# Loading the main part of wq in eight transfers of sixteen partitions instead of one of 128

## The chip, the cores and the metric

The kernel runs on one core of a Trainium2 chip. The metric is the device time of one execution in microseconds (us); for the kernel before it is 1275.67 us (median of 3 runs, 1275.54 to 1275.78). A change of 0.2% of that is 2.55 us.

## The reference

One token is decoded. It goes through a grouped-query attention over a long cache and, beside it, through a gated feed-forward block; a scalar gate mixes the two.

```python
x = A_x                                              # 1 x 1 x 448, bf16
g = _sigmoid((x * gate_w).sum(-1, keepdims=True))
a = _A_ref(x, k_cache, v_cache, wq, wo)              # 16 query heads of 256, 8 KV heads, 65536 positions
b = _B_ref(x, W_gate, W_up, W_down)                  # (relu(x W_gate) * (x W_up)) W_down, F = 1792
return g * a + (1 - g) * b
```

In `_A_ref` the queries are `q = x @ wq` (448 x 4096), then follow the scores against the K cache, a softmax over 65536 positions, the sum over the V cache and the product with `wo`. K and V are 8 x 65536 x 256 in bf16 each, 268 MB apiece. All weights together are some 12 MB.

## The kernel before, in words

All work is listed as operations with a key, an engine and the operations that they depend on (`_Plan`, the functions `op` and `dma`). Each engine runs its own operations in the order of their keys; `finish` turns the dependencies into waits on semaphores. Every engine has one counting semaphore; every DMA names one, which each transfer raises by 16, so an operation that depends on a transfer waits for the number that the semaphore has after that transfer.

The keys of the loads come from the list `order`, written out by hand, with a planned duration for each entry: wq, then the feed-forward weights, then the first K tile, then W_down, then K tiles and, from the fourth on, V tiles in turn; near the end the last V tiles in halves and pieces between the parts of wo. A K or V tile is 128 partitions x 64 KB, 8 MB, and there are 32 of each. They go through three buffers, `ring[0]` to `ring[2]`. A load is issued by SP (its DMA queue is q1 in the profile) and waits there until what its buffer held before has been used (`free`).

The weights of the start lie in the same buffers. `ring[2]` holds, per partition, three rows of wq (`wq3`, 24 KB), three rows of W_gate and three of W_up (10.5 KB each) and halves of the last rows of both; `ring[1]` holds the last 64 rows of wq as half rows (`wqa`, 4 KB per partition). With R3 = 3 and NR3 = 384, partition p of `wq3` holds the rows 3p, 3p+1 and 3p+2 of wq, which are contiguous in HBM.

The loads of the start are issued by two engines. SP issues, in this order: wq's main part (line 614), wq's rest (615), the rest of W_up (line 275), the first K tile into `ring[0]` (673). Behind these stands W_down (662), which waits for the queries, because it goes into the part of `ring[2]` that holds wq; the second K tile (`ring[1]`) waits for the queries too, the third (`ring[2]`) for the feed-forward block. ACT issues W_gate's main part (271), x (273), gate_w (274), the rest of W_gate (275) and W_up's main part (277) into its own queue, q10.

The queries are computed on TensorE. `f_q` (16 passes over three rows per partition, 48 matmuls) depends on the wq transfer (`l_["wq"]`), on x in its transposed form and, since operations that share a PSUM bank are kept in the order of their keys (`serialize`), on the scalar gate before it. The gate is a chain of small operations over POOL, DVE, ACT and PE that begins when x has landed. `f_q2` then adds the part of `wqa`. ACT copies the result, DVE transposes it and ACT builds `xm`, the stationary operand of all score matmuls.

In the main part DVE transposes each K tile in place (line 454), PE multiplies it with the queries (line 373, tile ST), DVE takes the maximum, ACT the exponentials, and after four tiles of a head the probabilities are rescaled and transposed and multiply the V tiles (line 373, tile O).

Of the kernel before, what the change touches and what calls it, by code (L numbers as in the profile page):

```python
# [25 lines left out]
class _Plan:  # L26
# [13 lines left out]
    def dma(self, eng, key, sem, fn, deps=()):  # L40
        if sem not in self.dsem:
            self.dsem[sem] = self.es.enter_context(self.nc.semaphore("d_" + sem))
        o = _Op(eng, key, fn, deps, dma=sem)
        self.ops.append(o)
        return o
# [66 lines left out]
def bass_gated_mix__gqa_block_cached__glu_gated_reglu__decode_kernel(  # L112
# [24 lines left out]
    R3 = D // 128  # L137
    NR3 = R3 * 128
# [13 lines left out]
    with es:  # L152
# [43 lines left out]
        wq3 = ring[2][:, 0:R3 * NQ]  # L196
# [21 lines left out]
        op, dma = pl.op, pl.dma  # L218
# [26 lines left out]
        t = 3.0  # L245
# [238 lines left out]
        l_, qk, smax, aexp, pv, last = {}, {}, {}, {}, {}, {}  # L484
# [126 lines left out]

        for kind, i, t in issue:
            if kind == "wq":
                l_["wq"] = dma("sp", t, "wq", lambda e: e.dma_start(wq3, A_wq[0:NR3, :].rearrange("(p k) n -> p (k n)", k=R3)))
                l_["wqh"] = dma("sp", t + 0.01, "wqh", lambda e: e.dma_start(
                    wqa, A_wq[NR3:D, :].rearrange("r (c n) -> (r c) n", c=2)))
                d_wh1 = dma("sp", t + 0.02, "wfh1", half(1, B_W_up))
# [8 lines left out]
            elif kind == "gu":  # L626
                t = tL["gu", 0]
# [41 lines left out]
            elif kind == "k":  # L669
                n = i  # L670
# [44 lines left out]
            elif kind in ("v", "vh", "vp"):  # L715
                if kind == "v":
                    n, lo, hi = i, 0, U
# [107 lines left out]
```

## Time and profile before

| | before |
|---|---|
| median of the runs | 1275.67 us |
| the profiled execution: its time | 1275.64 us |
| the profiled execution: its span | 1274.2 us |
| busy PE / DVE / ACT / POOL, share of the span | 29% / 51% / 5% / 3% |
| moved by DMA | 549.20 MB, mean 431 GB/s over the span |
| time of the packets of q1 / q10, share of 16 DMA engines' span | 99.2% / 0.6% |
| wq's main part, 3072 KB: issue to landing | 13.2 us |
| first K tile's issue by SP | at 2.11 us |
| first query matmuls on PE | at 18.20 us |

The span is the time from the first to the last instruction of the profiled execution on the core, and positions in it are given in us from its start. A row of the view of windows shows, for one stretch of the span, the busy time of each engine, the clock granted to PE, the share of the time that the core's 16 DMA engines were busy, and the rate at which they moved bytes. A packet is counted with its whole duration in the stretch in which it starts, so a stretch shorter than a few packets can show a share above 1. In the timeline, SPq and ACTq are the engines that issue transfers, with the duration of issuing one.

### The profile page before, as it was taken

To read this page: it belongs to the slowest core of one execution; us is meant where nothing else is said; L and a number is where in the kernel's file an instruction comes from. 1 tells how busy PE (TensorE), PEld (TensorE's weight loads), DVE (VectorE), ACT (ScalarE), POOL (GpSimd) and SP (SyncE) were. 2 spreads that over 40 slices of the span, in tenths; PEclk is the share of its full clock that TensorE was granted. 3 is DMA by queue.
4 is the path that set the end of the run, shared out by engine and by line. 5 is a ranking of instruction groups with operands and counts; after the bars stand their busy time and mean duration, and the time that the engine had idled before them with its cause. 6 is when DMAs were issued, how large, how long until landed. Compare 5 with 4: busy or idle time off the path is not lost.

```text
span 1274.2 us, 9555 instructions
## 1 busy us (share of the span) xinstructions
PE 371.4 (29%) x4483; PEld 105.0 (8%) x2909; DVE 648.7 (51%) x171; ACT 58.2 (5%) x112; POOL 37.2 (3%) x94
## 2 busy tenths in 40 slices
PE   4413222323133331224220342311332203223154
PEld 2101000101000000001000010000100000000010
DVE  1797633566534655445555454556535565336511
ACT  0000000000000000000000000000000000000000
POOL 2000000000000100001000010000100001000010
PEclk9566666656666665665656676556766556666577
DMA  9999999999999999999999999999999999999998
GB/s 414 429 444 428 426 428 430 447 438 428 428 432 428 442 435 434 428 434 428 441 434 434 428 434 430 439 434 434 428 438 428 436 434 434 430 438 428 436 421 378
DMA packets 11522, 549.20 MB, mean 431 GB/s; under 512 B 1267, under 2 KB 1654, under 8 KB 2422
## 3 DMA queue, kind: packets, MB, share of 16 engines
q1 hardware_dynamic: 11072, 546.05, 99.2%
q10 hardware_dynamic: 438, 2.98, 0.6%
q8 instruction: 8, 0.13, 0.0%
q14 instruction: 4, 0.03, 0.0%
HBM read 549.03 MB, written 0.00 MB: 431 GB/s over the span
## 4 chain that ended last, share of the span: by engine, by line
DMA 42%; DVE 32%; PE 16%; another core or an unknown queue 7%; issue 1%; POOL 0%; ACT 0%; SPq 0%; ACTq 0%
DMA ring<-in_A_k_cache_dram 34%; DVE ring L454 27%; PE ST L373 9%; PE O L373 5%; DMA ring<-in_A_v_cache_dram 4%; DMA ring<-in_A_wo_dram 3%; DVE P L701 1%; DVE P L699 1%; PE M_ps L373 1%; DVE o_sb L497 1%; DMA P<-in_A_x_dram 1%; DVE nmb L680 1%; PE ST L403 0%; PE M_ps L694 0%
## 5 line engine op out<-in xcount | busy, mean ns | idle before, releaser
L454 DVE STREAM_TRANSPOSE ring<-ring 128x16384 uint32<-128x16384 uint32 (+1 forms) x36 | 552.3, 15345 | 318.9 <-DMA ring<-in_A_k_cache_dram 318.9
L403 PE MATMUL ST<-nil_t,identb 1*128 1x1 bf16 x32 | 5.1, 158 | 767.6 <-DVE ring L454 767.6
L373 PE MATMUL ST<-ring,xm 128*16 x2048 | 185.2, 537 | 4.6 <-issue 0.7
L373 PE MATMUL O<-ring,P 128*32 x2016 | 133.9, 425 | 20.8 <-DMA ring<-in_A_v_cache_dram 18.3
L680 DVE TENSOR_REDUCE nmb<-ST 128x1 f32<-128x512 f32 x32 | 22.0, 688 | 185.0 <-PE ST L373 185.0
L682 ACT ACTIVATE P<-ST,nmb 128x512 bf16<-128x512 f32 x32 | 45.2, 1413 | 1082.8 <-DVE nmb L680 1082.8
L373 PEld LDWEIGHTS ST<-ring,xm 128*16 x2048 | 61.5, 112 | 115.2 <-issue 101.5
L403 PEld LDWEIGHTS ST<-nil_t,identb 1*128 1x128 bf16 x32 | 3.2, 100 | 792.6 <-issue 792.6
L497 DVE CAST_PREDICATED o_sb<-bm,O 128x512 bf16<-128x512 uint16 (+1 forms) x33 | 22.3, 679 | 69.2 <-PE O L356 46.9
L690 POOL TENSOR_TENSOR hs<-selc,hs 128x2 f32<-128x2 f32 x8 | 1.6, 196 | 1143.7 <-DVE hs L688 1143.7
L373 PEld LDWEIGHTS O<-ring,P 128*32 x504 | 15.7, 113 | 112.9 <-issue 110.4
L699 DVE TENSOR_TENSOR P<-P,hs 128x2048 bf16<-128x2048 bf16 x8 | 18.3, 2292 | 8.1 <-ACT hs L696 8.1
L702 POOL TENSOR_TENSOR hs<-hs,rs 128x4 f32<-128x4 f32 x8 | 18.4, 2305 | 13.6 <-ACT hs L696 13.6
L701 DVE STREAM_TRANSPOSE P<-P 128x2048 bf16<-128x2048 bf16 x8 | 18.5, 2311 | 0.3
L707 PE MATMUL M_ps<-hs,ones_f 128*128 128x2 f32 x16 | 4.7, 364 | 30.3 <-POOL hs L706 30.3
L373 PE MATMUL M_ps<-ring,P 128*128 x64 | 13.0, 341 | 1.5 <-PE M_ps L373 0.3
L525 PE MATMUL M_ps<-emat,o_sb 128*64 128x2 bf16 x48 | 3.0, 185 | 22.0 <-ACT o_sb L507 22.0
L682 ACT ACTIVATION_READ_ACCUMULATOR P<-ST,nmb 128x1 f32 x32 | 8.4, 263 | 0.0
L373 PEld LDWEIGHTS M_ps<-ring,P 128*128 x64 | 7.5, 119 | 6.9 <-issue 5.3
L336 DVE CAST xT<-M_ps 128x5 bf16<-128x5 f32 x1 | 0.2, 167 | 14.7 <-PE M_ps L324 14.7
L622 DVE STREAM_TRANSPOSE P<-P 128x128 uint32<-128x128 uint32 x1 | 0.3, 311 | 12.7 <-ACT P L621 12.7
L707 PEld LDWEIGHTS M_ps<-hs,ones_f 128*128 128x128 f32 x16 | 4.0, 312 | 30.9 <-POOL hs L706 30.9
(103 smaller groups left out, 94.0 us busy)
## 6 DMA issues: line engine op xcount, KB each, us to landing
ring<-in_A_v_cache_dram SPq DMA_DIRECT2D x3, 4096.0 KB, 28.9
ring<-in_A_v_cache_dram SPq DMA_DIRECT2D x2, 2048.0 KB, 36.3
ring<-in_A_wq_dram SPq DMA_DIRECT2D x1, 3072.0 KB, 13.2
ring<-in_A_wo_dram SPq DMA_DIRECT2D x1, 1792.0 KB, 19.6
ring<-in_B_W_down_dram SPq DMA_DIRECT2D x1, 1568.0 KB, 10.1
ring<-in_B_W_gate_dram ACTq DMA_DIRECT2D x1, 1344.0 KB, 13.4
ring<-in_B_W_up_dram ACTq DMA_DIRECT2D x1, 1344.0 KB, 26.5
ring<-in_A_wo_dram SPq DMA_DIRECT2D x1, 896.0 KB, 40.3
```

The costliest lines, as they stand in the source:

```text
L373: return e.add_instruction(mybir.InstMatmult(name=nc.get_next_instruction_name(), engine=e.engine, ins=[v, w], outs=[e.lower_ap(o)], start ...
L403: e.matmul(o, identb[0:1, :], nil_t[0:1, 0:1], start=True, stop=False, skip_group_check=True)
L454: return lambda e: e.transpose(v, v)
L497: return e.copy_predicated(dst, m.to_broadcast(list(src.shape)), src)
L525: ins = e.matmul(T_ps[p0:p0 + 64, s:c1 + 1:c1 - s], t[:, c:c + 64], emat2[:], start=(s == 0), stop=False, skip_group_check=True, tile_posi ...
L680: smax[n] = op("dv", tk + 26, lambda e, n=n, NM=NM, t_=t_: e.tensor_reduce(NM[:, t_:t_ + 1], ST[n % 2][:], AX.X, ALU.max, negate=True), [q ...
L682: aexp[n] = op("ac", tk + 27, lambda e, n=n, t_=t_, NM=NM, RS=RS, Ph=Ph: e.activation(Ph[:, t_:2048:4], ST[n % 2][:], ACTF.Exp, bias=NM[:, ...
L690: h2 = op("gp", T + 13.55, lambda e, X=X: e.tensor_tensor(X[:, 2:4], selc[:, 2:4], X[:, 0:1].to_broadcast([128, 2]), ALU.mult), [h1, g_sel])
L699: rsc = op("dv", T + 16, lambda e, X=X, pb=pb: e.tensor_tensor(pb, pb, X[:, 12:16].unsqueeze(1).to_broadcast([128, 512, 4]), ALU.mult), [h ...
L701: last["ev", h] = [op("dv", T + 17, lambda e, Ph=Ph: e.transpose(Ph[:], Ph[:]), [rsc])]
L702: l0 = op("gp", T + 18, lambda e, X=X, RS=RS: e.tensor_tensor(X[:, 16:20], X[:, 12:16], RS[:], ALU.mult), [h7])
L707: l3 = mop("pe", T + 19, lambda e, X=X: e.matmul(LS_ps, ones_f[:, :], X[:, 6:8], start=True, stop=True), [l2, c_one])
```

## The change

The transfer of wq's main part is replaced by eight. Transfer b (0 to 7) fills the sixteen partitions b, b+8, ..., b+120 of `wq3`, each with its same 24 KB from HBM. Their keys are 0.001 apart and lie ahead of the key of the next transfer, so SP issues all eight, one behind the other, before wq's rest. All eight raise the semaphore `wq`; `l_["wq"]` is the last of them, so the query matmuls wait until the semaphore has reached 128 instead of 16. Places, bytes and all other operations stay as they are.

```diff
             if kind == "wq":
-                l_["wq"] = dma("sp", t, "wq", lambda e: e.dma_start(wq3, A_wq[0:NR3, :].rearrange("(p k) n -> p (k n)", k=R3)))
+                wqs = A_wq[0:NR3, :].rearrange("(a b k) n -> a b (k n)", b=8, k=R3)
+                for b in range(8):
+                    l_["wq"] = dma("sp", t + 0.001 * b, "wq", lambda e, b=b: e.dma_start(wq3[b:128:8, :], wqs[:, b, :]))
                 l_["wqh"] = dma("sp", t + 0.01, "wqh", lambda e: e.dma_start(
                     wqa, A_wq[NR3:D, :].rearrange("r (c n) -> (r c) n", c=2)))
                 d_wh1 = dma("sp", t + 0.02, "wfh1", half(1, B_W_up))
```

## The prediction

> **What bounds the kernel now.** I began with the page's parts 2 and 3, to see whether anything but the transfers can set the end.
>
> ```profile
> DMA  9999999999999999999999999999999999999998
> GB/s 414 429 444 428 426 428 430 447 438 428 428 432 428 442 435 434 428 434 428 441 434 434 428 434 430 439 434 434 428 438 428 436 434 434 430 438 428 436 421 378
> ...
> q1 hardware_dynamic: 11072, 546.05, 99.2%
> q10 hardware_dynamic: 438, 2.98, 0.6%
> ```
>
> The 16 DMA engines are busy in every slice, and the packets of SP's queue (q1) and ACT's queue (q10) fill 99.8% of their time. The view of windows then shows where the remainder lies: the columns end with the DMA share and the GB/s.
>
> ```profile
> 0.00:1.70 1.70, 0.00 (x0) 0.00 (x0) 0.00 (x0) 0.00 (x0) 1.17 (x8) 1.00 0.00 0
> 1.70:3.60 1.90, 0.00 (x0) 0.00 (x0) 0.00 (x0) 0.63 (x1) 1.59 (x8) 1.00 0.89 252
> 3.60:12.80 9.20, 0.00 (x0) 0.00 (x0) 0.00 (x0) 0.66 (x1) 4.81 (x19) 1.00 1.00 431
> ...
> 100.00:1200.00 1100.00, 297.44 (x3795) 82.23 (x2422) 574.78 (x129) 49.21 (x92) 24.35 (x49) 0.62 1.00 433
> 1.70:1271.50 1269.80, 370.57 (x4473) 104.72 (x2901) 648.30 (x170) 57.85 (x111) 36.02 (x87) 0.63 1.00 432
> ```
>
> Nothing moves before 1.70 us, and from there to 1271.50 the share is 1.00. So the kernel is one unbroken stream of bytes with 1.7 us ahead of it and about 2.7 us behind it (1274.2 - 1271.5). A microsecond that the stream gains or loses anywhere, the start included, is a microsecond of the kernel, as long as the queues never run empty. The rate is also the same for very different rows: 431 GB/s where the rows of wq (24 KB) and W_gate (10.5 KB) run side by side, 433 where all are K and V rows of 64 KB. That is 26.9 GB/s for each engine (431 / 16), whatever the length: some fixed path is full, and row count or row length does not matter.
>
> SP's waits show what keeps the stream fed, and the timeline shows the issues at the start.
>
> ```profile
> SPq L719 <- PE ST L373: 912.1, 29, 36.0
> SPq L673 <- PE O L373: 156.7, 27, 13.9
> ...
> SPq L662 <- PE M_ps L373: 29.9, 1, 29.9
> ```
>
> ```profile
> 0.73 0.41 ACTq L271 DMA_DIRECT2D ring<-in_B_W_gate_dram  x1
> 0.74 0.38 SPq L614 DMA_DIRECT2D ring<-in_A_wq_dram  x1
> 1.18 0.42 SPq L615 DMA_DIRECT2D ring<-in_A_wq_dram  x1
> 1.64 0.42 SPq L275 DMA_DIRECT2D ring<-in_B_W_up_dram  x1
> 2.11 0.58 SPq L673 DMA_DIRECT2D ring<-in_A_k_cache_dram  x1
> ...
> 13.88 0.42 POOL L330 COPY P<-P 1x64 bf16<-1x64 bf16 x2 [4.28 <-DMA P<-in_A_x_dram]
> 18.20 7.94 PE L373 MATMUL M_ps<-ring,P 128*128 x48 [0.15 <-issue]
> 32.65 0.33 SPq L662 DMA_DIRECT2D ring<-in_B_W_down_dram  x1
> ```
>
> SP waits 29.9 us for the queries before it can issue W_down. That is the one place near the change where the stream could run dry. The next rows give the bytes ahead of it.
>
> ```profile
> ring<-in_A_wq_dram SPq DMA_DIRECT2D x1, 3072.0 KB, 13.2
> ring<-in_B_W_gate_dram ACTq DMA_DIRECT2D x1, 1344.0 KB, 13.4
> ring<-in_B_W_up_dram ACTq DMA_DIRECT2D x1, 1344.0 KB, 26.5
> ring<-in_A_wq_dram SPq DMA_DIRECT2D x1, 512.0 KB, 14.6
> ring<-in_B_W_up_dram SPq DMA_DIRECT2D x1, 224.0 KB, 18.0
> ring<-in_B_W_gate_dram ACTq DMA_DIRECT2D x1, 224.0 KB, 14.0
> ring<-in_B_W_down_dram SPq DMA_DIRECT2D x1, 1568.0 KB, 10.1
> ```
>
> The six loads ahead of W_down and the first K tile (8192 KB) are 14912 KB, 15.27 MB, or 35.4 us at 431 GB/s. The start lost 1.70 us and then 0.79 us (1.90 x (1 - 252/431)), so this stock lasts to 37.9 us. W_down is issued at 32.65, and by the first row of wq (issued 0.74, bytes at 1.7) its bytes can begin about 1.0 us later, at 33.7. The slack is 4.2 us.
>
> **The change part by part.**
>
> Issues. Seven more transfers on SP. One costs 0.44 to 0.47 us from start to start (0.74, 1.18, 1.64, 2.11), so wq's rest, W_up's rest and the first K tile are issued 3.1 to 3.3 us later, the K tile at about 5.4. What hides it: the stock of wq and W_gate rows, 4416 KB or 10.5 us of stream, ends near 13 us, well behind 5.4. The transfers of wq come fast enough too: an engine works through one of its wq rows and one W_gate row in 1.31 us (35328 B at 26.9 GB/s), SP brings the next in 0.47. Nothing else stands in SP's queue before 32.65. Cost 0; without that cover it would be 3.3 us. ACT's queue is untouched.
>
> Completion. Seven more completions per engine. The page has no row for one; from below it is 0, from above I take the whole gap between the stream's 432 GB/s and the slices' best 447, 3.4%, over wq's 7.3 us, which is 0.25 us. Most of that gap will have other reasons; I take 0.05.
>
> First rows. Each engine's first row ran at a reduced rate: share 0.89, but 252 GB/s. A transfer of 16 rows may be handed out to the engines sooner than one of 128. From below 0 (ACT's 128 rows are handed out at the same moment and the first row comes as late); from above all 0.79 us are won back. I take 0.2.
>
> The rows' own rate. This is the term that decides. [...] Every large transfer of the trace fills 128 partitions, so no row shows a store to a selection. The bounds are: no change, 0; and half rate, where the selection reaches only half of the paths and two rows share one, with wq's 3072 KB (3.146 MB) taking 14.6 us instead of 7.3, so +7.3. I take +7.3, nearer to what the rows tell of busy engines: in 1.70:3.60 they are 89% busy and yet move 252 of 431 GB/s, so an engine can be held up by something outside itself, and the same full-path rate for all row lengths is what a fixed store side would give. A gain by the selection has no row that speaks for it, since the rate is already the full one.
>
> [...]
>
> What is late next, if wq's rows take twice as long: an engine alternates between its two queues, so W_gate, and x behind it, are late as well. x lands 7.3 later at most, the gate chain that follows it (13.88 to 18.20) moves along, and the queries and W_down's issue with them, to 40.0. But the stock of bytes is late by the same 7.3, to 45.2, so the slack of 4.2 stays and adds nothing. If x were not late, wq's landing at about 21.2 would start the queries, 3.0 us later than now, with more slack still. The later loads have far more: the second K tile is issued right behind W_down, with 3.7 us of W_down ahead of it.
>
> Sum, against the profiled execution's 1275.64: +7.3 +0.05 -0.2 = 1282.8 us. The median of 1275.67 is 0.03 off that execution, which does not matter.
>
> **The rivals.**
>
> A, the selection costs nothing, because the engines alone are the full path. For it: 431 GB/s is 26.9 per engine in every stretch. Against: an engine can be busy and slow (252). Time 1275.64 + 0.05 - 0.2 = 1275.5, with bounds 1274.9 (all of 0.79 won back) and 1275.9. This is the side on which the kernel is not slower.
>
> [...]
>
> C, sharing leaves the engines uneven. Each landing counts when its last engine is through, and equal work afterwards does not even the lag out. If the last engine lags the mean by one doubled row (24576 B at half of 26.9 GB/s, 1.8 us), 1284.6.
>
> D, a transfer of sixteen rows does not run on sixteen engines. On eight, each would carry twice its rows of wq, so the time is +7.3 as well, but the DMA share would drop towards 0.5 in the stretch of wq. Nothing speaks for it: x's single small row tells nothing of its engines.
>
> **How the numbers follow.** About 0.2% (2.55 us) is what a measurement of this kernel can tell from no change. Half rate: 0.58, own range 1281.5 to 1284. A: 0.22. B: 0.08. C: 0.08. D: 0.02. The rest, 0.02, is left for a start that gains over 2.55 us in some way that I do not see. So faster 0.02, same 0.22 (A), slower 0.76. The range reaches from 1275.0, close to A's lower bound, to 1285.0, just beyond C; one sign holds most of the chance, but A is too likely to be left out.
>
> **What would show it.** In the stretch 3.60:12.80 the share stays 1.00 and the rate falls to about 254 GB/s (35328 B x 16 in 1.31 + 0.91 us); wq's landing moves from 13.9 to about 21, the queries from 18.2 to 21 to 25.5, W_down's issue to 36 to 40, and from 100 on everything runs at the old rate, shifted by 7. The rate back at 431 in that stretch shows A, a share well below 1 shows D or a hole from SP's issues, and zero windows around W_down's start show that the slack was spent. The prediction is wrong if the shift at 100 us is under 2.5 or over 10 us, or if it does not stay the same up to the end.

## The result and the profile after

The changed kernel takes 1283.95 us (median of 6 runs, 1283.68 to 1284.54) beside 1275.76 us for the kernel before in the same series. The ratio is 1.0065 with an interval of 1.0054 to 1.0076: 8.2 us slower, 1.2 us above the predicted 1282.8. The profiled execution took 1283.73 us with a span of 1282.3.

The view of windows of the changed kernel, for the stretches that the prediction named and the one behind them (the last columns are the DMA share and GB/s):

```profile
1.70:3.60 1.90, 0.00 (x0) 0.00 (x0) 0.00 (x0) 0.47 (x1) 1.59 (x8) 1.00 0.91 272
3.60:12.80 9.20, 0.29 (x5) 0.21 (x5) 0.43 (x2) 0.81 (x1) 5.69 (x22) 1.00 1.03 277
12.80:20.00 7.20, 0.58 (x2) 0.50 (x2) 3.27 (x11) 0.20 (x1) 0.96 (x3) 1.00 1.02 228
...
100.00:1200.00 1100.00, 299.13 (x3796) 81.77 (x2431) 574.32 (x130) 49.58 (x94) 24.36 (x49) 0.62 1.00 433
```

The engines are as busy as before (1.03 against 1.00), but between 3.6 and 12.8 us they move 277 GB/s instead of 431, and 228 in the next 7.2 us. From 100 us on the rate is the old 433. So the time is lost at the start, by busy engines, and nothing of it comes back. The stretch 3.60:12.80 is a mixture, because the first row of wq begins only at 5.2 us:

```profile
3.60:5.20 1.60, 0.00 (x0) 0.00 (x0) 0.00 (x0) 0.81 (x1) 1.29 (x5) 1.00 1.03 432
5.20:12.80 7.60, 0.29 (x5) 0.21 (x5) 0.43 (x2) 0.00 (x0) 4.40 (x18) 1.00 1.03 245
```

Until then W_gate's rows run alone at the full rate; with wq's rows among them the rate is 245.

The timeline of the changed kernel, with what answers to the lines shown of before:

```profile
0.74 5.28 SPq L616 DMA_DIRECT2D ring<-in_A_wq_dram  x8
...
7.16 0.43 SPq L675 DMA_DIRECT2D ring<-in_A_k_cache_dram  x1
...
10.56 0.42 POOL L330 COPY P<-P 1x64 bf16<-1x64 bf16 x2 [0.96 <-DMA P<-in_A_x_dram]
...
24.21 0.18 PE L403 MATMUL M_ps<-nil_t,identb 1*128 1x1 bf16 x1 [8.59 <-DMA ring<-in_A_wq_dram]
24.52 8.21 PE L373 MATMUL M_ps<-ring,P 128*128 x48
...
39.23 0.33 SPq L664 DMA_DIRECT2D ring<-in_B_W_down_dram  x1
```

The eight issues take SP 5.28 us. The operations that wait for x begin earlier than before (10.56 against 13.88), and the queries now wait 8.59 us for wq itself. W_down is issued at 39.23 instead of 32.65.

Whose rows took longer is seen in the view of the queues over the first 60 us, which gives packets, MB and the share of the 16 engines' time. ACT's queue carries the same bytes in these three kernels. First before, then the changed kernel, then the run with even and odd partitions (below), which loses nothing although its start too has ACT's rows ahead of wq's:

```profile
q10 hardware_dynamic: 436, 2.98, 11.9%
```

```profile
q10 hardware_dynamic: 436, 2.98, 16.2%
```

```profile
q10 hardware_dynamic: 436, 2.98, 12.8%
```

The packets of ACT's queue took 4.3% of 60 us more per engine than before, 2.6 us, although no transfer of this queue was changed. Of these, 0.9% or 0.5 us come with the other order at the start, since the even and odd partitions have them too; there wq's rows took 0.5 us less than before, so nothing was lost by it. The other 3.4%, 2.0 us, come with the sixteen-partition transfers. The durations of wq's own packets, added up and divided by the 16 engines, are 7.8 us before, 13.4 in the changed kernel and 7.3 with even and odd partitions. All packets together took 8.2 us per engine more than before, which is the whole loss.

### The profile page after: what moved, and what is told of

Same layout as the page of the kernel before. It is cut to its first block, busy times and chain, and to the rows that moved or that the text cites. A ratio compares the mean times of both kernels' runs of the same rounds, so it can differ in the third digit from the quotient of the medians.

```text
span 1282.3 us, 9562 instructions
## 1 busy us (share of the span) xinstructions
PE 371.8 (29%) x4483; PEld 104.3 (8%) x2909; DVE 648.8 (51%) x171; ACT 58.2 (5%) x112; POOL 37.2 (3%) x94
## 4 chain that ended last, share of the span: by engine, by line
DMA 44%; DVE 32%; PE 16%; another core or an unknown queue 6%; issue 1%; SPq 0%; ACT 0%; POOL 0%
DMA ring<-in_A_k_cache_dram 41%; DVE ring L454 27%; PE ST L373 9%; PE O L373 5%; DMA ring<-in_A_v_cache_dram 3%; DVE P L703 1%; DVE P L701 1%; DVE o_sb L497 1%; DVE nmb L682 1%; SPq L616 0%; PE ST L403 0%; PE M_ps L696 0%; ACT hs L698 0%; DVE mx L695 0%
## 5 line engine op out<-in xcount | busy, mean ns | idle before, releaser
L704 POOL TENSOR_TENSOR hs<-hs,rs 128x4 f32<-128x4 f32 x8 | 18.4, 2305 | 13.4 <-ACT hs L698 13.4
L624 DVE STREAM_TRANSPOSE P<-P 128x128 uint32<-128x128 uint32 x1 | 0.3, 311 | 21.2 <-ACT P L623 21.2
## 6 DMA issues: line engine op xcount, KB each, us to landing
ring<-in_A_wo_dram SPq DMA_DIRECT2D x1, 896.0 KB, 40.2
```

Of the source, the lines that this page charges most:

```text
L704: l0 = op("gp", T + 18, lambda e, X=X, RS=RS: e.tensor_tensor(X[:, 16:20], X[:, 12:16], RS[:], ALU.mult), [h7])
```

## The experiments

Four theories were set against each other: P, the write side is divided by partition number and the sixteen rows that run together share half of it; N, more and smaller transfers cost time as such; S, sixteen rows read at 192 KB steps from HBM are slow; Q, the loss comes from how late wq's first rows start. The number in front of each result is the median.

**The loss by itself: the same extra bytes, delivered in three ways.** Each of these kernels is the kernel before plus a second copy of wq's main part, in columns of `ring[1]` that nothing reads; `held` makes the second K tile wait for it (that line is not shown below). All work of the kernel before is still done. First by one transfer of 128 partitions:

```diff
+                l_["dum"] = dma("sp", t + 0.03, "dum", lambda e: e.dma_start(
+                    ring[1][:, 4096:4096 + R3 * NQ], A_wq[0:NR3, :].rearrange("(p k) n -> p (k n)", k=R3)))
```

> The kernel before, with wq's main part loaded once more, by one transfer of 128 partitions, into columns of ring[1] that nothing reads (the second K tile waits for it). It is the measure for the next two. Every theory: 3072 KB more at 431 GB/s, +7.3 us, 1283.0 us; the rate in its stretch stays near 431 GB/s.

Measured: 1283.06 us (before: 1276.03; ratio 1.0056, 1.004 to 1.0073). The extra bytes cost 7.0 us, near the 7.3 that 431 GB/s gives.

Then by eight transfers to every eighth partition:

```diff
+                wqs = A_wq[0:NR3, :].rearrange("(a b k) n -> a b (k n)", b=8, k=R3)
+                for b in range(8):
+                    l_["dum"] = dma("sp", t + 0.03 + 0.001 * b, "dum", lambda e, b=b: e.dma_start(
+                        ring[1][b:128:8, 4096:4096 + R3 * NQ], wqs[:, b, :]))
```

> As d_one128, but the extra copy comes by eight transfers of sixteen partitions, every eighth one, so the loss is measured away from the queries. Theory P (write paths go by partition number, and these sixteen rows meet in half of them): +7.3 for the bytes and 7 to 9 more, 1290 to 1292 us. Rival N (many small transfers, one row for an engine each, cost the time whatever their partitions): the same 1291. Rival S (sixteen rows read at 192 KB steps from HBM are slow): the same 1291. A rival Q, by which the loss comes from the late first rows of wq at the very start: 1283.

Measured: 1291.54 us (1.0121, 1.0104 to 1.0138), 8.5 us above the one transfer. Here wq itself starts as before, so Q falls: the loss needs no late first row.

Then the same eight sources, each to every fourth of 64 partitions in the middle:

```diff
+                for b in range(8):
+                    p, c = 32 + b % 4, 4096 + b // 4 * R3 * NQ
+                    l_["dum"] = dma("sp", t + 0.03 + 0.001 * b, "dum", lambda e, b=b, p=p, c=c: e.dma_start(
+                        ring[1][p:p + 64:4, c:c + R3 * NQ], wqs[:, b, :]))
```

> As d_every8, with the same eight transfers of the same sixteen rows from HBM, but each lands in the partitions p, p+4, ..., p+60 with p from 32 to 35, two transfers in different columns of the same partitions. Theory P: all paths are reached, one row in each, so the time is that of d_one128, 1283.0 within 1 us, with 24 KB rows near 431 GB/s. Rivals N and S: number, size and source of the transfers are those of d_every8, so the time is its 1291. [...]

Measured: 1283.07 us (1.0056, 1.0039 to 1.0073), 0.01 us from the one transfer of 128. Number, size, source and issue of the transfers are those of the run before it; only the destination partitions (and, with them, the columns) differ, and 8.5 us are gone. N and S fall with that, and the eight completions cost nothing that can be measured. The windows of the two show it directly; first every eighth, then every fourth partition:

```profile
20.00:26.00 6.00, 5.97 (x41) 4.46 (x39) 0.38 (x4) 0.00 (x0) 0.00 (x0) 1.00 1.04 219
24.00:32.00 8.00, 6.66 (x34) 3.02 (x31) 0.00 (x0) 0.00 (x0) 0.00 (x0) 0.87 1.07 224
```

```profile
20.00:26.00 6.00, 6.00 (x41) 4.72 (x39) 0.54 (x5) 0.00 (x0) 0.00 (x0) 1.00 1.08 462
24.00:32.00 8.00, 6.61 (x36) 3.19 (x34) 0.00 (x0) 0.00 (x0) 0.00 (x0) 0.90 1.13 485
```

The engines are fully busy in both, at 219 and 224 GB/s in one and at 462 and 485 in the other. (Figures above 433 come from counting a packet where it starts.)

**A steady stretch.** To see what a doubled row costs without its surroundings (doubled: by P, two of the rows that run together share one path), the eight extra transfers were made twice, `for b in range(16)` with `b % 8` as the selection and a second set of columns.

> As d_every8, with the eight extra transfers made twice (sixteen, into two sets of columns). It separates what a doubled row costs in a steady stretch from what is paid once, where the doubled rows meet others. d_every8 took 1291.5, 8.5 more than d_one128, while half rate alone is 7.3. If the rest of 1.2 is paid once: the second eight add 7.3 for their bytes and 7.3 for half rate, 1306.1. If it goes with the rows: 7.3 + 8.5, 1307.3. If the loss as a whole were paid once: 1298.8.

Measured: 1306.23 us (1.0238, 1.0221 to 1.0255). That is 14.7 above the run with eight, so the second eight cost 7.3 for their bytes and 7.4 for the lost rate. The rate over 22 us, which in this kernel these rows alone fill; then the same stretch of the kernel with the single transfer of 128, where it is the last rows of that copy and K rows of 64 KB:

```profile
24.00:46.00 22.00, 10.09 (x63) 3.25 (x44) 4.01 (x5) 2.49 (x9) 0.00 (x0) 0.68 1.00 215
```

```profile
24.00:46.00 22.00, 11.09 (x71) 4.04 (x53) 4.01 (x5) 2.49 (x9) 0.00 (x0) 0.73 0.99 430
```

215 is half of 430. The single packets say the same: a row of 24 KB took 1.82 us in the mean in these sixteen transfers and 0.92 in the one transfer of 128. So half rate is exact in a steady stretch. Of the 8.5 us that d_every8 loses against d_one128, 7.5 are in the rows of wq and its copy. Another 0.6 are in the first sixteen K rows, which begin while the last doubled rows run: 3.06 us each against 2.42. In d_twice8 this is again 0.6 and not twice as much, so it is paid once per stretch. The run's time alone could not show that, since its four runs lie 1.4 us apart.

**Other selections in the place of the change.** wq's main part in two transfers, partitions 0 to 63 and 64 to 127:

```diff
+                wqs = A_wq[0:NR3, :].rearrange("(b a k) n -> a b (k n)", b=2, k=R3)
+                for b in range(2):
+                    l_["wq"] = dma("sp", t + 0.001 * b, "wq", lambda e, b=b: e.dma_start(wq3[64 * b:64 * b + 64, :], wqs[:, b, :]))
```

> wq's main part by two transfers, partitions 0 to 63 and 64 to 127. Theory P: each reaches half of the write paths, as the eight transfers did, so the loss is the same 7 to 9 us, 1283 to 1285. Rival N (number of transfers): one transfer more instead of seven, 8.2 / 7 = 1.2 us, 1276.9. Rival S (source at 192 KB steps): the source rows lie together, no loss, 1275.7.

Measured: 1283.91 us (1.0063, 1.0046 to 1.008). Two large transfers of neighbouring partitions lose as much as the change with its eight.

The even and the odd partitions (`"(a b k) n -> a b (k n)", b=2` and `wq3[b:128:2, :]`):

> wq's main part by two transfers, the even and the odd partitions. Theory P: the sixty-four rows of a transfer reach all paths, so it depends on which of them the engines take at one time: 1275.7 if these spread over all paths, 1284 if the engines take neighbouring rows one after the other, so that sixteen rows at steps of eight partitions run together. Rival N: 1276.9. Rival S: between 1275.7 and 1284.

Measured: 1276.05 us, ratio 1.0001 (0.9991 to 1.0011). Same number and size of transfers as the halves, and no loss: what counts is which partitions are reached together. The windows of the stretch in which wq is loaded, first the halves, then the even and odd ones:

```profile
3.60:12.80 9.20, 0.00 (x0) 0.00 (x0) 0.00 (x0) 0.81 (x1) 4.78 (x19) 1.00 1.04 265
```

```profile
3.60:12.80 9.20, 0.29 (x5) 0.21 (x5) 1.03 (x3) 0.96 (x2) 6.21 (x22) 1.00 1.02 435
```

Eight transfers of sixteen neighbouring partitions (`"(b a k) n -> a b (k n)", b=8` and `wq3[16 * b:16 * b + 16, :]`):

> wq's main part by eight transfers of sixteen neighbouring partitions. Theory P: each transfer reaches a quarter of the paths, four rows in one: 29.2 us for wq instead of 7.3 if all engines stay in step (+21.9, 1297.6), less where transfers in neighbouring blocks overlap; in any case more than the change itself, 1288 to 1298. Rival N (same number and size of transfers as the change): 1284. Rival S: the source rows lie together, 1275.7.

Measured: 1295.87 us (1.0158, 1.0141 to 1.0175), 20.0 us lost, near the 21.9 of a quarter of the rate. Its windows where wq's rows run almost alone (1.57 of the 1.80 MB from 16 to 32 us):

```profile
16.00:24.00 8.00, 0.29 (x5) 0.21 (x5) 0.43 (x2) 0.00 (x0) 0.42 (x2) 1.00 0.93 112
20.00:26.00 6.00, 0.29 (x5) 0.21 (x5) 1.03 (x3) 0.20 (x1) 1.43 (x3) 1.00 0.86 103
24.00:32.00 8.00, 0.58 (x2) 0.49 (x2) 3.26 (x11) 0.20 (x1) 1.42 (x3) 1.00 0.94 113
```

A quarter of 431 is 108. So the rate goes in steps with the selection: the full 430 to 431 with 128 partitions (the even and odd ones met 435, the middle ones by four 462 to 485), 215 with every eighth one, 103 to 113 with blocks of sixteen neighbours. The halves stand at 265 with W_gate's rows among theirs, and their time is that of the change (1283.91 and 1283.95). All five selections agree with P. No trace shows a path itself, and of other selections nothing is shown.

**Can the loss be spread away?** Each transfer of d_every4 reached eight partitions of the remainder b by 8 and eight of b + 4 (b from 0 to 3), at 462 to 485 GB/s, where sixteen of one remainder ran at 219 and 224 (d_every8). So, by P, the selections b and b + 4 of the change do not share their half of the paths. The changed kernel with its transfers in the order 0, 4, 1, 5, 2, 6, 3, 7:

> [...] Rivals N and S: nothing about the transfers differs but their order, 1284.

Measured: 1283.75 us (1.0062, 1.0045 to 1.0078), as the change itself. By P, an engine at b and one that is a row ahead, at b + 4, would then not meet. The landings in the trace show how far apart they are: wq's transfers land 128 times, sixteen for each transfer. Taken in order, sixteen at a time, these landings lie within 0.6 to 0.8 us of each other in the changed kernel (the last two groups within 1.4 and 1.6), and within 1.1 to 1.7 with this order (the last two within 2.0 and 2.8). So the engines spread more and still nothing was won. Which of them write by the same path the trace does not say, so whether those stay together is open. Then the transfers b = 0 to 3 on SP, those with b = 4 to 7 on ACT ahead of W_gate (`f_q` waits for both; only the part for ACT is shown):

```diff
+                for b in range(4, 8):
+                    l_["wq2"] = dma("ac", -11 + 0.001 * b, "wq2", lambda e, b=b: e.dma_start(wq3[b:128:8, :], wqs[:, b, :]))
```

> [...] Rivals N and S: 1284.

Measured: 1282.37 us (1.0049, 1.0033 to 1.0066), 6.6 us above before and 1.6 below the change (1283.95): most of the loss stays with the two queues too. No run here beats the kernel before; the nearest, with even and odd partitions, is the same within 0.1%.

## Why the prediction was right

**What bounds the kernel.** As said: the stream of transfers has no room, so what it loses at the start is the kernel's loss. The last row of each of the first five K and V tiles ends 8.2 us later than before (at 38 to 120 us of the kernel before), and from there to the end of the stream the shift stays between 7.9 and 8.2.

**Issues.** Mis-sized, without effect. One issue of sixteen partitions was to cost 0.44 to 0.47 us, as those in the trace of before; a line's own view of the changed kernel shows the durations of the eight, with minimum, median and maximum in ns:

```profile
L616 SPq DMA_DIRECT2D ring<-in_A_wq_dram x8: 567/592/774, 0.7 to 5.4; - x8
```

The first K tile was issued at 7.16, not 5.4. The cover named, the stock of wq and W_gate rows, held all the same: the packets fill 1279.9 of the 1280.2 us from the first to the last byte (before: 1271.7 of 1272.1), so the engines did not run out of rows. d_every4 has eight such issues too and pays nothing, though wq's first copy gives it more cover.

**Completion.** 0.05 taken, at most 0.25. The pair of d_one128 and d_every4 shows 0.01, which cannot be told from zero.

**First rows.** 0.2 taken of at most 0.79. The stretch 1.70:3.60 moved 272 instead of 252 GB/s, 1.90 x 20 / 431 = 0.1 us. But 264 to 269 are found there in d_one128, d_every8 and d_every4, whose first transfers are those of the kernel before, so no gain by the change is shown.

**The rows' own rate.** The choice of the far bound was right, and its 7.3 is exact for a steady stretch (215 GB/s). The half itself was the author's estimate: nothing in the trace of before shows it, nor that rows share paths; what the runs show is the rate, 215 of 430 in d_twice8. The term was too small for this place, by 0.9 (8.2 against 7.3). It counted only wq's rows and took the rows beside them at full rate. Against the run with even and odd partitions, whose start has the same order, wq's rows took 6.1 us more per engine, less than 7.3, and ACT's rows 2.0. So rows that run beside doubled rows are slower too; the forecast of 254 GB/s, which left them at full speed, met 245. In d_every8 the rows that paid were K rows. Where the time lies is shown; why the sum comes out above 7.3 was not settled. The forecast of 1282.8 is 1.2 off mostly by this term and by the 0.2 for first rows that is not seen; 1283.95 lies at the upper end of its own range for half rate (1281.5 to 1284).

**What is late next.** The step said that x would be late with W_gate. It was early: in the first 5 us the changed kernel's view of the queues has packets of ACT's queue alone, where before SP's had 0.79 MB.

```profile
q10 hardware_dynamic: 102, 1.10, 62.0%
```

```profile
q1 hardware_dynamic: 32, 0.79, 47.4%
q10 hardware_dynamic: 26, 0.28, 14.0%
```

So W_gate ran first and wq after it. Then the other branch held, in which wq's landing starts the queries, but at 24.2 instead of 21.2, as its rows also began 3.4 us later (5.2 against 1.8). The conclusion stands: W_down's issue at 39.23 was inside the 36 to 40, and the stock lasted to 46.0 (37.9 + 8.1, the shift of the span), 5.8 us beyond 40.2.

**The rivals.** A falls with d_every8 against d_every4. B, that engines which drift apart lose less than the full 7.3, falls with the loss of 8.2 itself; the alternating order took 0.2 us off it (1283.95 - 1283.75), the two queues 1.6 (8.2 - 6.6). C falls with the landings: of the changed kernel's wq transfers the last sixteen lie within 1.6 us, but those of the first K tile within 0.65, against 0.62 before, and those of the last loads within 1.8 in both. So a lag arose and did not last, and the 8.2 us are in the mean of the engines, not in the last one. D falls with the share of 1.03 in the stretch of wq, all 16 engines.

## What to carry to other kernels

In these runs a transfer's rate depends on which partitions the rows that run together land in, not on how many transfers there are: compare the GB/s of its stretch at a DMA share of 1.00 with that of a full 128-partition transfer (430 here), and a half or a quarter (215 and 103 to 113 here) points to this cause. If a load must be split, choose a selection whose rate was seen to stay full: here the even and odd partitions (1276.05 beside 1275.91) and the middle ones by four (1283.07 beside 1283.06 for one transfer). In a kernel that is one unbroken stream, price such a loss by the bytes at the lost rate, and add something for the rows that run beside or right behind them (2.0 and 0.6 us here).

## What was not expected of the hardware

Where wq was split into even and odd partitions, halves or every eighth one, its first rows came only after about 5 us, although SP issued the first transfer at 0.74; in their place W_gate's rows filled the engines. With one transfer of 128 or blocks of sixteen neighbours SP's rows came first (its queue moved 0.79 MB in the first 5 us before and 0.39 with the blocks, and none in the changed kernel, the halves and the even and odd partitions). Before and in the changed kernel the queue came first whose first issue was over first: before, SP's at 1.12 and ACT's at 1.14; in the changed kernel ACT's at 1.12 and SP's at 1.35. Whether this is what decides, and why SP's rows then wait until 5 us, is open; it costs nothing (even and odd: 1276.05 beside 1275.91).

Issuing sixteen partitions at a step of eight took SP 0.59 us in the median, against 0.38 for 128 partitions in a row. The step alone does not decide this: sixteen neighbours took 0.42 in the median (blocks16), 64 neighbours 0.57 (halves64).

Neither the alternating order nor two queues won much back (1283.75 and 1282.37), although the landings show the engines further apart with the alternating order than in the changed kernel. Why is open.
